# Ordering the attention output's small matrix products by tile size, and issuing two scalar loads from GpSimd

## The chip, the cores and the metric

The kernel runs on one core of one Trainium2 chip. The metric is the device time of one execution in microseconds. A core has the engines TensorE (PE in the profile, its weight loads PEld), VectorE (DVE), ScalarE (ACT), GpSimd (POOL) and SyncE (SP), which here issues nearly all DMA transfers.

## What is computed

A gated linear attention with a running 48 x 48 state per head is followed by a two-layer network with a squared ReLU. There are 4 batches of 8 heads, 768 steps, 48 channels a head; the network takes the 3072 x 384 result through a 2048-wide layer and back.

```python
for t in range(S):
    state = alpha[:, :, t, :, None] * state + einsum('bhd,bhe->bhde', k[:, :, t], v[:, :, t])
    y[:, :, t] = einsum('bhd,bhde->bhe', q[:, :, t], state)
x = y.transpose(0, 2, 1, 3).reshape(B * S, H * D)      # 3072 x 384
r = maximum(x @ w_in, 0)
out = (s * (r * r) + b) @ w_out                        # s and b are scalars
```

## The kernel before

**Blocks.** The 768 steps of a batch are cut into 6 chunks of 128, so there are 24 blocks of 128 steps (blocks 0, 6, 12 and 18 open a batch and have no state yet). For each block the attention runs through these steps:

- `load` (L175): four DMA transfers (alpha, q, k, v) into rings of 5 buffers, issued from SP.
- `st_ln` (L275, ACT): logarithm of alpha into one of two buffers `la`. `st_cum` (L281, L286, PE): running sums over the block into the PSUM tile `ct_ps`. `st_exp_b`, `st_exp_i` (L295 to L299, ACT): exponentials `b_s`, `binv`, `blast`.
- `st_qb`, `st_kb` (L308, L313, DVE): scaled q and k. `st_T` (L324, PE): eight transposes, `st_Tcopy` (L344, DVE) copies them out to `qkT`.
- `st_vcast` (L302, POOL): v in bf16 into one of three buffers `vp`. `st_KV` (L335, PE): eight products of k and v into the PSUM tile `py_ps`. `st_t1` (L354, L356, DVE) and `st_snew` (L364, POOL): the next state `s_st`.
- `st_A` (L370, PE): eight products of k and q into `a_ps`. `st_mask` (L379, DVE): the causal mask, into `am`.
- `st_y` (L409, L419, PE): the block's output, transposed, into `py_ps`. `st_yevac` (L433, ACT): copies it to `xd`.

**The y products.** The output of 4 pairs of 96 channels lies as 384 channels in 12 strips of 32 PSUM partitions (strip x is in column block x // 4, at partition 32 * (x % 4)). A pair of heads fills 3 strips, so its products are 64 and 32 columns wide. `S_PARTS` lists the 8 products of the state with q (L409, left out where the block opens a batch) and `V_PARTS` the 12 products of v with the masked scores (L419). In order, the widths are 64, 32, 32, 64, 64, 32, 32, 64 for the state, and 64, 32, 32, 64, 64, 32, 32, 64, 32, 32, 32, 32 for v. Each product has a weight load of its own (128 rows, 64 or 32 columns) and streams 128 columns.

**The network.** Blocks are gathered in groups (2, 2, 2, 2, 4, 4, 4, 4 blocks). `mm1` (L455, PE) writes into `h_ps`, `relu` (L464, ACT) and `square` (L472, DVE) follow, `mm2` (L479, PE) accumulates into `o_ps`, `oevac` (L490, DVE) applies s and the bias row, and `ostore` (L502, SP) writes out. The bias row is b times the column sums of w_out: `colsum_part` and `colsum_add` (L247, L252, DVE), `bias_mul` (L255, L256, POOL, which waits for `b_col`) and `bias_mm` (L262, PE).

**What sets the order.** Every step is entered in a planner (`Schedule`) with an engine, an estimated duration, a priority and the data it reads and writes. The planner runs the list with these estimates, and each engine's instructions are emitted in the order that comes out; on the chip each engine then keeps to that order. For loads, the planner knows that block 0's four inputs come at 3.5 to 6.5 us (`sched.done`, L527), and takes 0.98 us of SP time and 2 us of latency for each later load. The `st_y` of a block stands in it at 0.6 us (L582). The output stores stand on SP too, in the order in which the planner sees them become ready.

Of the kernel before, what the change touches and what calls it, by code (L numbers as in the profile page):

```python
# [114 lines left out]
def kernel(  # L115
# [12 lines left out]
    nc = tc.nc  # L128
# [23 lines left out]
    y_ps = py_ps[:, 0:384].rearrange("a (k t) -> a k t", k=3)  # L152
# [17 lines left out]
    s_col = sb.tile([128, 1], FP32, name="s_col")  # L170
# [219 lines left out]
    def quadrant(x):  # L390
        return x // 4, 32 * (x % 4)

    S_PARTS = [(0, 0, 2), (0, 2, 1), (1, 3, 1), (1, 4, 2), (2, 6, 2), (2, 8, 1), (3, 9, 1), (3, 10, 2)]
    V_PARTS = [
        (0, 0, 0, 2), (0, 1, 2, 1), (1, 0, 3, 1), (1, 1, 4, 2), (2, 0, 6, 2), (2, 1, 8, 1),
        (3, 0, 9, 1), (3, 1, 10, 2), (0, 1, 1, 1), (1, 0, 4, 1), (2, 1, 7, 1), (3, 0, 10, 1),
    ]

    def st_y(n):
        first = n % NCH == 0  # L400
        qT = qkT_sb[n % 2][:, 0]
        am = am_sb[n % 2]
        vp = vp_sb[n % 3]
        st = s_sb[(n - 1) % 2]
        if not first:
            for p, x, m in S_PARTS:
                kk, r0 = quadrant(x)
                c0 = 32 * x - 96 * p
                nc.tensor.matmul(  # L409
                    out=y_ps[r0 : r0 + 32 * m, kk, :],  # L410
                    lhsT=st[:, p, c0 : c0 + 32 * m],
                    rhs=qT[:, p, :],
                    start=(x < 4),
                    stop=False,
                )
        for i, (p, e, x, m) in enumerate(V_PARTS):
            kk, r0 = quadrant(x)
            c0 = 32 * x - 96 * p + 48 * e
            nc.tensor.matmul(  # L419
                out=y_ps[r0 : r0 + 32 * m, kk, :],  # L420
                lhsT=vp[:, p, c0 : c0 + 32 * m],
                rhs=am[:, e, p, :],
                start=(first and i < 3),
                stop=(i >= 8),
            )
# [80 lines left out]
    op = sched.op  # L506
# [15 lines left out]
    for rank, item in enumerate(loads):  # L522
        t, i = rank - 1000, int(item[1:])
        if item[0] == "b":
            if i == 0:
                for x, name in enumerate("aqkv"):
                    sched.done((name, 0), 3.5 + x)  # L527
                op("SP", 0.5, t + 0.5,
                   lambda: nc.sync.dma_start(out=b_col, in_=moe_b.to_broadcast((128, 1))),
                   w=["b"], lat=2.0)  # L530
                op("SP", 0.5, t + 0.6,
                   lambda: nc.sync.dma_start(out=s_col, in_=moe_s.to_broadcast((128, 1))),
# [3 lines left out]
        st = stage % NST  # L536
# [15 lines left out]
    for g in range(NG):  # L552
        m = GROUPS[g]
        ring = [(first_blk[g] + x) % RING for x in range(m)]
        for n in range(first_blk[g], first_blk[g] + m):
# [26 lines left out]
            op("PE", 0.6, t + 0.7, st_y, n, r=rr, w=["py"], lat=0.27)  # L582
# [57 lines left out]
```

## Time and profile before

| | us |
|---|---|
| median of 3 runs | 233.87 |
| lowest, highest | 233.66, 234.86 |
| the profiled execution's own time | 235.56 |
| its span in the profile | 233.8 |
| TensorE busy in the span | 211.7 |
| VectorE busy | 144.0 |
| ScalarE busy | 100.8 |
| GpSimd busy | 45.4 |

The profile is of one execution on the one core. Its page lists the busy time of each engine, the span in 40 slices, and the chain of work that ended last, followed back from the last instruction. Other views give instructions in order of time (start, duration, engine, line, what is written from what, count; several alike in a row are merged), the busy time of each engine in chosen stretches (with the number of its instructions that lie in the stretch in brackets), and who waited for whom. A duration of a matrix product is from its start to the modelled end of its drain, so products overlap in the rows, and the distance between starts is what a product costs TensorE.

### The profile page before, as it was taken

Reading aid. Unit: us, or ns where it says so; the run is one execution under the profiler, and the core shown is the slowest. Engines: PE = TensorE matmul, PEld = TensorE weight load, DVE = VectorE, ACT = ScalarE, POOL = GpSimd, SP = SyncE. Lnnn points to the kernel's source line nnn. Section 1 sums busy time; section 2 is a strip of 40 time slices with the busy share of each in tenths; the row PEclk is TensorE's granted clock in tenths of the full one; section 3 lists DMA queues with packets and bytes.
Section 4 is the critical chain, followed back from the end, with each engine's and each line's share of the span. In section 5 each row is a group of like instructions: output and inputs, shape, how many; then the busy total and the mean of one; then the engine's idle time right before and its main releaser. Section 6 shows DMA issues by size and latency. Waiting matters only on the chain.

```text
span 233.8 us, 4929 instructions
## 1 busy us (share of the span) xinstructions
PE 211.7 (91%) x1916; PEld 123.9 (53%) x1916; DVE 144.0 (62%) x283; ACT 100.8 (43%) x217; POOL 45.4 (19%) x63
## 2 busy tenths in 40 slices
PE   0268696799999999999999999999999999999993
PEld 0134473466676666655555555545555555555562
DVE  2266459998779666675767865597656754343321
ACT  3213351554565534523656545675354433444300
POOL 5234439333102220200202120001210100000000
PEclk9999999799999999999999999999999999999999
DMA  6999798995789989689895464300000100101111
GB/s 135 184 289 249 199 366 197 242 205 111 157 171 213 192 190 185 143 172 215 170 181 101 97 146 104 67 3 34 35 3 34 36 0 34 36 35 38 64 70 67
DMA packets 107320, 30.21 MB, mean 129 GB/s; under 512 B 100640, under 2 KB 105760, under 8 KB 107296
## 3 DMA queue, kind: packets, MB, share of 16 engines
q1 hardware_dynamic: 107296, 29.89, 55.2%
q8 instruction: 15, 0.25, 0.5%
q14 instruction: 9, 0.07, 0.1%
HBM read 25.17 MB, written 4.72 MB: 128 GB/s over the span
## 4 chain that ended last, share of the span: by engine, by line
PE 82%; SPq 7%; DVE 5%; DMA 3%; issue 1%; ACT 0%
PE h_ps_67 L455 14%; PE o_ps_69 L479 14%; PE h_ps_66 L455 14%; PE o_ps_68 L479 13%; PE py_ps L419 8%; PE py_ps L409 7%; SPq L175 5%; PE ct_ps L324 4%; PE a_ps L370 3%; PE py_ps L335 3%; DMA a_in_73<-in_alpha_dram 3%; PE ct_ps L281 2%; SPq L220 1%; DVE colpart L247 1%; DVE colsum L252 1%
## 5 line engine op out<-in xcount | busy, mean ns | idle before, releaser
L464 ACT ACTIVATE r_149<-h_ps_66 128x512 bf16<-128x512 f32 x48 | 28.7, 598 | 46.2 <-PE h_ps_66 L455 37.4
L455 PEld LDWEIGHTS <-w_in_bf 128*128 128x128 bf16 x384 | 34.9, 100 | 22.0 <-issue 2.1
L464 ACT ACTIVATE r_150<-h_ps_67 128x512 bf16<-128x512 f32 x48 | 28.7, 599 | 20.1 <-PE h_ps_67 L455 13.5
L455 PE MATMUL h_ps_66<-xd_147,w_in_bf 128*128 128x512 bf16 (+1 forms) x72 | 17.0, 357 | 0.0
L379 DVE TENSOR_TENSOR am_138<-a_ps,mask 128x1024 bf16<-128x1024 f32 x12 | 14.7, 1222 | 3.4 <-PE a_ps L370 3.2
L344 DVE COPY qkT_136<-ct_ps 128x1024 bf16<-128x1024 bf16 x12 | 8.3, 688 | 13.7 <-PE ct_ps L324 13.7
L455 PE MATMUL h_ps_67<-xd_147,w_in_bf 128*128 128x512 bf16 (+1 forms) x72 | 16.5, 348 | 0.0
L344 DVE COPY qkT_137<-ct_ps 128x1024 bf16<-128x1024 bf16 x12 | 8.3, 690 | 12.9 <-PE ct_ps L324 12.8
L379 DVE TENSOR_TENSOR am_139<-a_ps,mask 128x1024 bf16<-128x1024 f32 x12 | 14.7, 1221 | 2.3 <-PE a_ps L370 2.0
L455 PE MATMUL h_ps_67<-xd_146,w_in_bf 128*128 128x256 bf16 (+1 forms) x72 | 13.8, 321 | 1.5 <-ACT r_150 L464 1.5
L455 PE MATMUL h_ps_66<-xd_146,w_in_bf 128*128 128x256 bf16 (+1 forms) x72 | 13.9, 323 | 0.0
L364 POOL TENSOR_TENSOR s_st_144<-t_142,blast_140 128x384 bf16<-128x384 bf16 x8 | 7.7, 968 | 24.6 <-DVE t_142 L356 17.7
L433 ACT ACTIVATE xd_147<-py_ps 128x384 bf16<-128x384 f32 x10 | 4.9, 490 | 15.2 <-PE py_ps L419 15.2
L409 PE MATMUL py_ps<-qkT_137,s_st_144 128*64 128x128 bf16 (+1 forms) x96 | 11.4, 242 | 0.0
L324 PE MATMUL ct_ps<-ident_bf,qb_128 128*128 128x128 bf16 x48 | 5.1, 234 | 5.4 <-DVE qb_128 L308 5.4
L409 PEld LDWEIGHTS <-s_st_144 128*64 128x64 bf16 (+1 forms) x96 | 6.2, 101 | 6.9 <-issue 3.5
L455 PE MATMUL h_ps_66<-xd_148,w_in_bf 128*128 128x256 bf16 (+1 forms) x48 | 9.8, 327 | 0.0
L455 PE MATMUL h_ps_67<-xd_148,w_in_bf 128*128 128x256 bf16 (+1 forms) x48 | 9.8, 327 | 0.0
L364 POOL TENSOR_TENSOR s_st_145<-t_143,blast_141 128x384 bf16<-128x384 bf16 x8 | 7.0, 879 | 13.3 <-DVE t_143 L356 11.2
L419 PEld LDWEIGHTS <-vp_113 128*32 128x32 bf16 (+1 forms) x96 | 5.0, 99 | 6.3 <-issue 3.5
L281 PE MATMUL ct_ps<-la_97,U_bf 128*128 128x384 bf16 x12 | 4.5, 376 | 4.1 <-ACT la_97 L275 4.1
L295 ACT ACTIVATE b_s_125<-ct_ps 128x384 f32<-128x384 f32 x12 | 5.9, 489 | 5.4 <-PE ct_ps L286 5.1
(207 smaller groups left out, 480.8 us busy)
## 6 DMA issues: line engine op xcount, KB each, us to landing
out_dram<-o_sb_167 SPq DMA_DIRECT2D x8, 192.0 KB, 2.0
out_dram<-o_sb_168 SPq DMA_DIRECT2D x8, 192.0 KB, 2.0
out_dram<-o_sb_169 SPq DMA_DIRECT2D x8, 192.0 KB, 1.9
a_in_70<-in_alpha_dram SPq DMA_DIRECT2D x5, 192.0 KB, 4.2
q_in_75<-in_q_dram SPq DMA_DIRECT2D x5, 192.0 KB, 3.6
k_in_80<-in_k_dram SPq DMA_DIRECT2D x5, 192.0 KB, 3.9
v_in_85<-in_v_dram SPq DMA_DIRECT2D x5, 192.0 KB, 4.0
a_in_71<-in_alpha_dram SPq DMA_DIRECT2D x5, 192.0 KB, 3.6
```

What stands on the lines that cost most here:

```text
L175: nc.sync.dma_start(out=dst[n % NIN], in_=src[b, :, c * C : (c + 1) * C, :].rearrange("h s d -> s h d"),)
L281: nc.tensor.matmul(out=cum_ps, lhsT=U_bf, rhs=la[:, :, 0:D], start=True, stop=True)
L324: nc.tensor.transpose(out=t_ps[:, x, p, :], in_=f[:, 128 * p : 128 * p + 128], identity=ident_bf,)
L335: nc.tensor.matmul(out=p_ps[64 * e : 64 * e + 64, p, :], lhsT=kb[:, 128 * p + 64 * e : 128 * p + 64 * e + 64], rhs=vp[:, p, 48 * e : 48 * ...
L344: nc.vector.tensor_copy(out=qkT_sb[n % 2].rearrange("a x p t -> a (x p t)"), in_=t_ps.rearrange("a x p t -> a (x p t)"),)
L364: nc.gpsimd.tensor_tensor(out=s_sb[n % 2], in0=t1_sb[n % 2], in1=bl, op=ALU.mult)
L379: nc.vector.tensor_tensor(out=am_sb[n % 2].rearrange("a e p t -> a (e p) t"), in0=a_ps.rearrange("a e p t -> a (e p) t"), in1=mask.unsquee ...
L409: nc.tensor.matmul(out=y_ps[r0 : r0 + 32 * m, kk, :], lhsT=st[:, p, c0 : c0 + 32 * m], rhs=qT[:, p, :], start=(x < 4), stop=False,)
L419: nc.tensor.matmul(out=y_ps[r0 : r0 + 32 * m, kk, :], lhsT=vp[:, p, c0 : c0 + 32 * m], rhs=am[:, e, p, :], start=(first and i < 3), stop=( ...
L455: nc.tensor.matmul(out=hp[:, i * n : (i + 1) * n], lhsT=w_in_bf[:, kk, 128 * j : 128 * (j + 1)], rhs=xd_sb[g % 3][:, kk, 0:n], start=(kk = ...
L464: nc.scalar.activation(out=r_sb[w % 2], in_=h_ps[w % 2], func=AF.Relu)
L479: nc.tensor.matmul(out=op[:, 0:d_model], lhsT=gt_sb[j][:, c0 : c0 + C], rhs=w_out_bf[:, j, :], start=(j == 0), stop=(j == NJ - 1),)
```

## The change

The two lists become one, `Y_PARTS`, in which all products 64 columns wide come first (four of the state, four of v) and then all products 32 columns wide (four of the state, eight of v). Neighbours in the list go to different partitions: two products of 64 columns, or four of 32, fill the 128 output partitions. The products themselves, their number and their sizes stay. Which product starts the accumulation in a strip is now worked out from the order. The two loads of the scalars b and s are issued from GpSimd in place of SP, in the planner too, and the planner's estimate of `st_y` goes from 0.6 to 0.55 us.

```diff
-    S_PARTS = [(0, 0, 2), (0, 2, 1), (1, 3, 1), (1, 4, 2), (2, 6, 2), (2, 8, 1), (3, 9, 1), (3, 10, 2)]
-    V_PARTS = [
-        (0, 0, 0, 2), (0, 1, 2, 1), (1, 0, 3, 1), (1, 1, 4, 2), (2, 0, 6, 2), (2, 1, 8, 1),
-        (3, 0, 9, 1), (3, 1, 10, 2), (0, 1, 1, 1), (1, 0, 4, 1), (2, 1, 7, 1), (3, 0, 10, 1),
+    Y_PARTS = [
+        (0, None, 0, 2), (2, None, 6, 2), (1, None, 4, 2), (3, None, 10, 2),
+        (0, 0, 0, 2), (2, 0, 6, 2), (1, 1, 4, 2), (3, 1, 10, 2),
+        (2, None, 8, 1), (3, None, 9, 1), (0, None, 2, 1), (1, None, 3, 1),
+        (2, 1, 8, 1), (3, 0, 9, 1), (0, 1, 2, 1), (1, 0, 3, 1),
+        (1, 0, 4, 1), (0, 1, 1, 1), (3, 0, 10, 1), (2, 1, 7, 1),
     ]
...
+        parts = [x for x in Y_PARTS if not (first and x[1] is None)]
+        fresh = {0, 1, 2, 3}
+        for i, (p, e, x, m) in enumerate(parts):
+            c0 = 32 * x - 96 * p
+            mine = {(x + y) % 4 for y in range(m)}
+            start = mine <= fresh
+            fresh -= mine
...
-                op("SP", 0.5, t + 0.5,
-                   lambda: nc.sync.dma_start(out=b_col, in_=moe_b.to_broadcast((128, 1))),
+                op("POOL", 0.5, t + 0.5,
+                   lambda: nc.gpsimd.dma_start(out=b_col, in_=moe_b.to_broadcast((128, 1))),
                    w=["b"], lat=2.0)
-                op("SP", 0.5, t + 0.6,
-                   lambda: nc.sync.dma_start(out=s_col, in_=moe_s.to_broadcast((128, 1))),
+                op("POOL", 0.5, t + 0.6,
+                   lambda: nc.gpsimd.dma_start(out=s_col, in_=moe_s.to_broadcast((128, 1))),
                    w=["s"], lat=2.0)
...
-            op("PE", 0.6, t + 0.7, st_y, n, r=rr, w=["py"], lat=0.27)
+            op("PE", 0.55, t + 0.7, st_y, n, r=rr, w=["py"], lat=0.27)
```

Three places of the emitted order matter for the prediction. The first is TensorE at the y products of block 0, which opens a batch and has the 12 products of v alone; `vp_113` is its v, `am_138` its masked scores, and the last numbers are the output partitions by the streamed columns. Before, from its first product on:

```order
L419 LDWEIGHTS vp_113
L419 MATMUL py_ps<-am_138,vp_113 64x128
L419 LDWEIGHTS vp_113
L419 MATMUL py_ps<-am_138,vp_113 32x128
L419 LDWEIGHTS vp_113
L419 MATMUL py_ps<-am_138,vp_113 32x128
L419 LDWEIGHTS vp_113
L419 MATMUL py_ps<-am_138,vp_113 64x128
```

With the change, from the third product on (the two ahead of it are 64 wide as well):

```order
L414 LDWEIGHTS vp_113
L414 MATMUL py_ps<-am_138,vp_113 64x128
L414 LDWEIGHTS vp_113
L414 MATMUL py_ps<-am_138,vp_113 64x128
L414 LDWEIGHTS vp_113
L414 MATMUL py_ps<-am_138,vp_113 32x128
L414 LDWEIGHTS vp_113
L414 MATMUL py_ps<-am_138,vp_113 32x128
```

The width changed at every first, third and fifth product of a run of four; now it changes once in the block, after the last product that is 64 wide.

The second place is the start, on ACT, where `la_97` is the logarithm of block 0's alpha and `la_99` that of block 1's, and on POOL, where `vp_113` is block 0's v and `vp_115` block 1's. On ACT:

```order
-L635 UNCONDITIONAL_BRANCH
+L634 UNCONDITIONAL_BRANCH
 L184 ACT_TABLE_LOAD
+L275 ACTIVATE la_99<-a_in_71 128x8x48
 L275 ACTIVATE la_97<-a_in_70 128x8x48
```

On POOL:

```order
+L528 DMA b_col<-in_moe_b_dram 128x1
+L531 DMA s_col<-in_moe_s_dram 128x1
 L255 MEMSET bones 128x128
 L256 TENSOR_SCALAR bones<-bones,b_col 128x128
+L302 CAST vp_115<-v_in_86 128x4x2x48
 L302 CAST vp_113<-v_in_85 128x4x2x48
-L302 CAST vp_115<-v_in_86 128x4x2x48
```

The two loads stand ahead of the instruction that reads b, and on both engines block 1's step now stands ahead of block 0's, because the planner takes block 1's loads to land before block 0's.

The third place is SP's queue, around the store of block 1's output (`o_sb_168`) and the loads of block 9 (`a_in_74` to `v_in_89`) and block 10 (`a_in_70`). Before:

```order
L175 DMA v_in_88<-in_v_dram 128x8x48
L502 DMA out_dram<-o_sb_168 128x384
L175 DMA a_in_74<-in_alpha_dram 128x8x48
L175 DMA q_in_79<-in_q_dram 128x8x48
L175 DMA k_in_84<-in_k_dram 128x8x48
L175 DMA v_in_89<-in_v_dram 128x8x48
L175 DMA a_in_70<-in_alpha_dram 128x8x48
```

With the change:

```order
L175 DMA v_in_88<-in_v_dram 128x8x48
L175 DMA a_in_74<-in_alpha_dram 128x8x48
L175 DMA q_in_79<-in_q_dram 128x8x48
L175 DMA k_in_84<-in_k_dram 128x8x48
L175 DMA v_in_89<-in_v_dram 128x8x48
L175 DMA a_in_70<-in_alpha_dram 128x8x48
L501 DMA out_dram<-o_sb_168 128x384
```

The store moved behind five loads.

30 lines of the change are left out of this document (9 added, 21 removed).

## The prediction

> **What bounds the kernel now.** I read the page first (the span, the busy shares, the granted clock), then the chain of work that ended last, then the busy times of chosen stretches, then the instructions in order of time around one block's y products.
>
> ```profile
> span 233.8 us, 4929 instructions
> PE 211.7 (91%) x1916; PEld 123.9 (53%) x1916; DVE 144.0 (62%) x283; ACT 100.8 (43%) x217; POOL 45.4 (19%) x63
> PE h_ps_67 L455 14%; PE o_ps_69 L479 14%; PE h_ps_66 L455 14%; PE o_ps_68 L479 13%; PE py_ps L419 8%; PE py_ps L409 7%; SPq L175 5%; PE ct_ps L324 4%; PE a_ps L370 3%; PE py_ps L335 3%; DMA a_in_73<-in_alpha_dram 3%; PE ct_ps L281 2%; SPq L220 1%; DVE colpart L247 1%; DVE colsum L252 1%
> ```
>
> TensorE is busy for 91% of the span and makes up most of the chain. The y products (L409 and L419) are about 15% of it, some 35 us. The chain in order of time (start, duration, what) shows where TensorE starts to be the bound:
>
> ```profile
> 18.16 6.32 DMA a_in_73<-in_alpha_dram
> ...
> 30.46 0.85 PE py_ps L409 x8
> ...
> 41.29 1.13 DVE am_139 L379
> ...
> 49.49 0.76 PE h_ps_67 L455 x6
> ...
> 53.56 0.85 PE py_ps L409 x8
> ...
> 195.94 0.85 PE py_ps L409 x8
> ...
> 227.61 2.61 PE o_ps_69 L479 x16
> ```
>
> Up to 24.5 us the chain is SP and its transfers, then TensorE with block 2's y (30.46), then VectorE until some 49 us, and from 49.49 us on TensorE to the end. Blocks 4 (53.56) to 23 (195.94) have their y in that last stage: 20 blocks, of which 6, 12 and 18 open a batch, so 17 with 20 products and 3 with 12. What a y costs TensorE there is paid in full. Two stretches (columns: PE, PEld, DVE, ACT, POOL busy, granted clock, DMA share) show how much room the others have:
>
> ```profile
> 50.00:60.00 10.00, 10.00 (x105) 6.49 (x103) 9.17 (x23) 5.32 (x14) 3.75 (x4) 1.00 0.74 154
> ...
> 81.86:89.13 7.26, 7.26 (x80) 4.81 (x80) 5.06 (x13) 3.62 (x9) 1.33 (x2) 1.00 0.92 192
> ```
>
> The second is one block's period. VectorE works 5.06 of 7.26 us in it, ScalarE 3.62. In the first, just after the VectorE stage, VectorE has little room (9.17 of 10). The clock is granted in full.
>
> **What a y costs now.** In order of time, block 14's y (20 products) and what follows it, and block 6's y (12 products):
>
> ```profile
> 125.87 0.92 PE L409 MATMUL py_ps<-qkT_136,s_st_145 128*64 128x128 bf16 x8
> ...
> 127.57 0.82 PE L455 MATMUL h_ps_66<-xd_147,w_in_bf 128*128 128x512 bf16 x3
> ```
>
> ```profile
> 68.02 1.09 PE L419 MATMUL py_ps<-am_138,vp_113 128*64 128x128 bf16 x12
> 69.04 0.28 PE L455 MATMUL h_ps_67<-xd_148,w_in_bf 128*128 128x256 bf16 x1
> ```
>
> So a y costs 127.57 - 125.87 = 1.70 us, and 69.04 - 68.02 = 1.02 us in a block that opens a batch. Cutting block 14's y into stretches of 0.17 us shows how it comes about (the busy time and number of the weight loads, each of which goes with one product):
>
> ```profile
> 125.86:126.03 0.17, 0.11 (x1) 1.00 0.00 0
> 126.03:126.20 0.17, 0.10 (x2) 1.00 0.00 0
> 126.20:126.37 0.17, 0.11 (x2) 1.00 0.23 48
> ...
> 127.22:127.39 0.17, 0.11 (x1) 1.00 1.17 220
> 127.39:127.56 0.17, 0.10 (x4) 1.00 1.25 256
> ```
>
> The products go in 10 steps of 0.17 us: one 64 wide, two 32 wide, two 64 wide and so on to four 32 wide (the five stretches left out hold 2 each). Every step is a run of equal width, and the step costs 0.17 us whether it holds one product, two or four. Products of one width on different partitions run beside each other; where the width changes, TensorE stands. A block that opens a batch has 6 such steps, 6 x 0.17 = 1.02 us, as measured.
>
> What a step without a change of size costs is in the rows of the transposes and of the score products, all streaming 128 columns:
>
> ```profile
> 128.23 0.39 PE L324 MATMUL ct_ps<-ident_bf,qb_130 128*128 128x128 bf16 x4
> 128.45 0.39 PE L324 MATMUL ct_ps<-ident_bf,kb_134 128*128 128x128 bf16 x4
> ...
> 123.23 0.40 PE L370 MATMUL a_ps<-qkT_136 64*128 64x128 bf16 x8
> 123.56 0.34 PE L281 MATMUL ct_ps<-la_99,U_bf 128*128 128x384 bf16 x1
> ```
>
> Four transposes take 128.45 - 128.23 = 0.22 us, 0.055 us each. The eight score products take 0.33 us up to the next size: they go in four pairs, three steps of 0.055 and one of 0.165 us that holds the change. So 0.055 us is streaming and some 0.115 us the change of size.
>
> **The change part by part.**
>
> *The y order.* A full y becomes four pairs of 64 and then three rows of four 32: three steps of 0.055, one of 0.17 (64 to 32), two of 0.055, one of 0.17 (32 to the next size): 0.62 us. It saves 1.08 us. A y that opens a batch becomes two pairs and two rows of four: 0.055 + 0.17 + 0.055 + 0.17 = 0.45 us; it saves 0.57 us. In the last stage that is 17 x 1.08 + 3 x 0.57 = 20.1 us. The trace has a row of four 32-wide products only once in a block, with a change behind it; that three of them follow at 0.055 us each is taken over from the pairs. The bounds are 0.62 us and, if each of the seven steps cost 0.17 us, 7 x 0.17 = 1.19 us; I take 0.62, since the pairs are the nearest row. The Trainium skill speaks against it in one place: TensorE: Matmul & The Clock Gate, section "Wait — 56ns, not 53.3ns?", gives about 62 ns of sequencer time for each product with hardware decode off. By it 20 products take an estimated 1.24 us, and the sum would be 17 x 0.46 + 3 x 0.28 = 8.7 us. The score products above do not agree with it: 8 in 0.33 us, the change included, are 0.041 us each.
>
> *What comes next where TensorE is faster.* A block's period goes from 7.26 to about 6.2 us. VectorE's 5.06 us fit (82%). In the stretch from 50 to 60 us TensorE would need 10 - 1.08 = 8.9 us (block 4's y lies in it), while VectorE has 9.17 us to do: 0.3 us come back. For queueing behind VectorE elsewhere I add 0.9 us, a choice: 1.2 us, with bounds of 0 and 6 us (0.3 us for each of the 20 blocks).
>
> *The scalar loads and the start.* In order of time:
>
> ```profile
> 3.45 0.98 SPq L529 DMA_DIRECT2D b_col<-in_moe_b_dram  x1
> 3.49 0.52 ACT L275 ACTIVATE la_97<-a_in_70 128x384 bf16<-128x384 f32 x1 [1.50 <-DMA a_in_70<-in_alpha_dram]
> ...
> 4.34 0.29 PE L286 MATMUL ct_ps<-ones_col_bf,la_97 128*128 128x1 bf16 x4
> ...
> 5.11 0.60 SPq L175 DMA_DIRECT2D a_in_71<-in_alpha_dram  x1
> ...
> 7.48 0.50 POOL L302 CAST vp_113<-v_in_85 128x384 bf16<-128x384 f32 x1
> ...
> 8.46 0.52 ACT L275 ACTIVATE la_99<-a_in_71 128x384 bf16<-128x384 f32 x1 [4.45 <-DMA a_in_71<-in_alpha_dram]
> 8.89 0.47 ACT L295 ACTIVATE b_s_124<-ct_ps 128x384 f32<-128x384 f32 x1
> ...
> 11.02 0.53 PE L335 MATMUL py_ps<-vp_113,kb_132 128*64 128x96 bf16 x8
> 11.14 0.51 POOL L302 CAST vp_115<-v_in_86 128x384 bf16<-128x384 f32 x1 [3.16 <-DMA v_in_86<-in_v_dram]
> ```
>
> ```profile
> 5.00:6.00 1.00, 0.00 (x0) 0.00 (x0) 0.00 (x0) 0.00 (x0) 0.00 (x0) 1.00 0.58 107
> 6.00:7.00 1.00, 0.00 (x0) 0.00 (x0) 0.00 (x0) 0.00 (x0) 0.07 (x1) 1.00 0.36 52
> ```
>
> SP issues b and s from 3.45 us, and block 1's first load follows at 5.11: without them every later load moves up by up to 1.66 us. The transfers can use that only while they idle; from 5 to 7 us they are busy 0.58 and 0.36, so about 1.06 us of them is free. The early chain is SP and transfers, so I take 1.0 us. The bounds: 2.7 us gained (1.66 and block 2's 1.08, which stands on the chain at 30.46), and 1 us lost.
>
> Loss could come from the swapped steps. On ACT block 1's logarithm now stands ahead of block 0's. It waited for its load until 8.46; the exponential behind it came at 8.89, though block 0's sums were done by 4.63 (4.34 + 0.29). Now block 0's logarithm starts 0.43 us behind block 1's, and the exponential 1.1 us behind that (4.63 - 3.49): with the load 1.66 us earlier, 6.80 + 0.43 + 1.14 = 8.4 us, against 8.89. Nothing is lost while that load gains 1.1 us or more of its 1.66. On POOL, both casts of v now wait behind `bones`, which waits for b, and block 0's behind block 1's. Block 0's k-v products (11.02) need it. With v of block 1 some 1.5 us earlier, the casts end at about 10.6 us, so b has until some 9.5 us to land, 5.6 us after POOL reaches its issue at about 3.9. No row has a transfer issued from GpSimd; the nearest is SP's b, 0.98 us of issue. By DMA: Bandwidth & Descriptors, section "Anatomy of one DMA — SWDGE (gpsimd) path", of the Trainium skill a GpSimd transfer takes about 2.0 us fixed, an estimate of 6 us for the landing; no run here shows it yet. Either way it costs nothing.
>
> *The planner's order.* The loads of block 9 were the tightest in the last stage:
>
> ```profile
> 63.97 0.36 SPq L502 DMA_DIRECT2D out_dram<-o_sb_168  x1
> 64.42 0.38 SPq L175 DMA_DIRECT2D a_in_74<-in_alpha_dram  x1
> ...
> 68.67 0.51 ACT L275 ACTIVATE la_99<-a_in_74 128x384 bf16<-128x384 f32 x1
> ```
>
> The load went out behind the store at 64.42 and was used at 68.67. The new order puts five loads ahead of that store, so a shorter period does not run into it. I cost the reordering at nothing; where the tight loads came late after all, it is in the 6 us above.
>
> **The sum.** 20.1 + 1.0 - 1.2 = 19.9 us less. The profiled execution took 235.56 us, 1.8 more than its span, and would take 215.7. It lies 1.7 us above the median of the runs, 233.87; against that the forecast is 214.0 us. About 0.5%, 1.2 us, is what a measurement here can tell from no change.
>
> **The rivals.**
>
> *A. No row of products follows the next without a stall.* If the weights of a row of equal width are not loaded beside the row ahead, each of the seven steps costs 0.17 us: a y of 1.19 us saves 0.51, one that opens a batch (4 x 0.17 = 0.68) 0.34 us, 9.7 us in all, about 224. Against it stand the score products, whose pairs follow at 0.055 us; for it, that no three rows of four follow each other in the trace. A limit on how fast products are issued would show the same way, a y of over 1 us; its chance is in this one. Chance 0.10.
>
> *B. VectorE or the loads take over.* For it: 9.17 of 10 us at the start of the stage, and the load used 4.25 us after its issue. Against it: 5.06 of 7.26 us later, and the new SP order. At 0.2 to 0.35 us a block, 4 to 7 us come back: 218 to 221. Chance 0.14.
>
> *C. Slower: weight loads go one by one.* All y products use all 128 rows. The Trainium skill says (TensorE: Matmul & The Clock Gate, Part 3, "The mechanism") that a weight load overlaps running products only where the row group differs. Here it would work so: at about 0.10 us a load (the 0.10 and 0.11 of the stretches), 20 loads and two changes of 0.115 are 2.2 us a y, 0.5 us more than now, and 12 loads 1.4 us, 0.4 more: 17 x 0.5 + 3 x 0.4 = 10 us, about 243. It decides where a load costs over (1.70 - 0.23) / 20 = 0.073 us. Against it: four loads lie within 0.10 us in the last stretch, and the score products go at 0.041 us each. The trace thus does not agree with that rule for different columns. Chance 0.03.
>
> *D. Nothing to measure*, if VectorE bound the whole last stage at today's pace. Its 5.06 of 7.26 us speak against it. Chance 0.02, at 234.
>
> **How the numbers follow.** The forecast has 0.71: 214.0 us, with its own bounds about 210.5 (no time comes back, 2.7 us gained early: 233.87 - 20.1 - 2.7 = 211.1, and half a microsecond of spread) and 217. B reaches to 221. The range 210.5 to 221.5 holds the forecast and B, 0.85, less some at their edges; A, C and D lie outside. Faster: forecast, A and B, 0.95. Within 0.5%: 0.02. Slower: C, 0.03.
>
> **What would show it.** Right: after the change a y costs 0.6 to 0.65 us from its first product to the next line, with loads in one stretch of four pairs and one of twelve; PE's busy time falls by 20 us or more; TensorE still has no wait from some 50 us on; the first transfer of block 1 is issued at about 3.5 us. Wrong: a y over 0.8 us (A or C); waits of TensorE on `am`, `gt` or `a_in` between 50 and 190 us that add up to over 3 us (B); a first k-v product later than 11.5 us (the start lost, not gained).

## The result and the profile after

| | before | after |
|---|---|---|
| median, us | 234.06 (4 runs, 233.66 to 234.86) | 217.59 (4 runs, 215.89 to 220.06) |
| ratio, 95% interval | | 0.9268 [0.9207, 0.9329] |
| the profiled execution | 235.56, span 233.8 | 217.64, span 215.9 |

The changed kernel is 16.5 us faster by the medians; 19.9 us had been forecast, to 214.0. The run of 220.06 is left out of the ratio, and so is one of 983.64 us of after_again below, because each lies over 1.5% above the fastest run of its kernel.

From the page of the changed kernel, the span, the busy time of each engine and the granted clock in 40 slices:

```profile
span 215.9 us, 4933 instructions
PE 190.6 (88%) x1916; PEld 112.4 (52%) x1916; DVE 149.3 (69%) x283; ACT 100.8 (47%) x217; POOL 47.5 (22%) x65
PEclk9999998788999999999999999999999999999999
```

TensorE's busy time falls from 211.7 to 190.6 us, by 21.1. Its clock dips in slices 7 to 10, between 32 and 54 us.

In order of time, block 14's y (20 products) and what follows it:

```profile
118.92 0.30 PE L414 MATMUL py_ps<-qkT_136,s_st_145 128*64 128x128 bf16 x4
119.05 0.28 PE L414 MATMUL py_ps<-am_138,vp_117 128*64 128x128 bf16 x4
119.26 0.24 PE L414 MATMUL py_ps<-qkT_136,s_st_145 128*32 128x128 bf16 x4
119.33 0.28 PE L414 MATMUL py_ps<-am_138,vp_117 128*32 128x128 bf16 x8
119.55 0.61 PE L454 MATMUL h_ps_66<-xd_147,w_in_bf 128*128 128x512 bf16 x2
```

A full y takes 119.55 - 118.92 = 0.63 us, where it took 1.70. Its two halves are 0.34 (64 wide) and 0.29 us (32 wide).

The busy times in three stretches (columns as before: PE, PEld, DVE, ACT, POOL busy, granted clock, DMA share):

```profile
50.00:60.00 10.00, 10.00 (x113) 6.72 (x110) 9.30 (x23) 6.46 (x15) 3.02 (x4) 0.98 0.64 134
...
100.00:120.00 20.00, 19.78 (x225) 10.07 (x224) 17.66 (x33) 15.00 (x34) 4.14 (x6) 1.00 0.80 163
112.80:118.90 6.10, 6.10 (x69) 3.09 (x68) 5.09 (x11) 4.71 (x10) 1.61 (x2) 1.00 0.66 130
```

From 50 us on TensorE is the bound as before: in a block's period, now 6.10 us, it is busy all the time and VectorE 5.09 us. Of TensorE's waits only one lies behind 50 us, the 0.22 us that are missing between 100 and 120.

The start, in order of time:

```profile
3.75 0.86 SPq L175 DMA_DIRECT2D a_in_71<-in_alpha_dram  x1
3.83 0.74 POOL L528 DMA_DIRECT2D b_col<-in_moe_b_dram  x1
4.57 0.55 POOL L531 DMA_DIRECT2D s_col<-in_moe_s_dram  x1
...
7.21 0.61 POOL L256 TENSOR_SCALAR bones<-bones,b_col 128x128 f32<-128x128 f32 x1 [1.89 <-DMA b_col<-in_moe_b_dram]
...
8.13 0.52 ACT L275 ACTIVATE la_99<-a_in_71 128x384 bf16<-128x384 f32 x1 [6.13 <-DMA a_in_71<-in_alpha_dram]
...
9.72 0.49 ACT L295 ACTIVATE b_s_124<-ct_ps 128x384 f32<-128x384 f32 x1 [0.65 <-PE ct_ps L286]
...
11.58 0.50 POOL L302 CAST vp_113<-v_in_85 128x384 bf16<-128x384 f32 x1
...
12.13 0.53 PE L335 MATMUL py_ps<-vp_113,kb_132 128*64 128x96 bf16 x8 [0.20 <-POOL vp_113 L302]
```

```profile
5.00:6.00 1.00, 0.00 (x0) 0.00 (x0) 0.00 (x0) 0.00 (x0) 0.33 (x2) 1.00 0.93 181
6.00:7.00 1.00, 0.00 (x0) 0.00 (x0) 0.00 (x0) 0.00 (x0) 0.00 (x0) 1.00 0.90 172
```

Block 1's alpha load went out 1.36 us earlier (3.75 against 5.11), yet was used only 0.33 us earlier (8.13 against 8.46): the transfers, 0.58 and 0.36 busy between 5 and 7 us before, were now 0.93 and 0.90 busy. These are single executions, and y_issue below shows the same load gain more. Block 0's exponential, now behind block 1's logarithm, came 0.83 us later (9.72 against 8.89), and its first k-v products 1.1 us later (12.13 against 11.02).

So the y products are as forecast, and 3.4 us of the sum (19.9 - 16.5) are missing elsewhere. The theory at this point: the y order is worth what was forecast, and the move of the scalar loads, with the new order that the planner makes of it, costs time. The rivals: the y order gives less than its shorter products say, or the swapped steps at the start cost it.

### The profile page after: what moved, and what is told of

The parts are those of the page before. It is cut to its first block, busy times and chain, and to the rows that moved or that the text cites. A ratio compares the mean times of both kernels' runs of the same rounds, so it can differ in the third digit from the quotient of the medians.

```text
span 215.9 us, 4933 instructions
## 1 busy us (share of the span) xinstructions
PE 190.6 (88%) x1916; PEld 112.4 (52%) x1916; DVE 149.3 (69%) x283; ACT 100.8 (47%) x217; POOL 47.5 (22%) x65
## 4 chain that ended last, share of the span: by engine, by line
PE 51%; DVE 0%; issue 0%
PE o_ps_69 L478 10%; PE h_ps_66 L454 10%; PE o_ps_68 L478 10%; PE h_ps_67 L454 10%; PE py_ps L414 3%; PE ct_ps L324 2%; PE a_ps L370 2%; PE py_ps L335 2%; PE ct_ps L281 1%; PE ct_ps L286 0%; DVE o_sb_169 L489 0%
## 5 line engine op out<-in xcount | busy, mean ns | idle before, releaser
L454 PEld LDWEIGHTS <-w_in_bf 128*128 128x128 bf16 x384 | 36.0, 102 | 23.9 <-issue 3.1
L454 PE MATMUL h_ps_66<-xd_147,w_in_bf 128*128 128x512 bf16 (+1 forms) x72 | 16.3, 344 | 1.4 <-ACT r_149 L463 1.4
L454 PE MATMUL h_ps_67<-xd_147,w_in_bf 128*128 128x512 bf16 (+1 forms) x72 | 16.7, 352 | 0.0
L454 PE MATMUL h_ps_67<-xd_146,w_in_bf 128*128 128x256 bf16 (+1 forms) x72 | 14.4, 333 | 0.7 <-ACT r_150 L463 0.7
L454 PE MATMUL h_ps_66<-xd_146,w_in_bf 128*128 128x256 bf16 (+1 forms) x72 | 15.0, 344 | 0.0
L364 POOL TENSOR_TENSOR s_st_144<-t_142,blast_140 128x384 bf16<-128x384 bf16 x8 | 7.7, 960 | 23.5 <-DVE t_142 L356 16.3
L364 POOL TENSOR_TENSOR s_st_145<-t_143,blast_141 128x384 bf16<-128x384 bf16 x8 | 7.8, 974 | 15.4 <-DVE t_143 L356 13.3
L454 PE MATMUL h_ps_66<-xd_148,w_in_bf 128*128 128x256 bf16 (+1 forms) x48 | 9.8, 327 | 0.0
L454 PE MATMUL h_ps_67<-xd_148,w_in_bf 128*128 128x256 bf16 (+1 forms) x48 | 9.8, 326 | 0.0
L295 ACT ACTIVATE b_s_124<-ct_ps 128x384 f32<-128x384 f32 x12 | 5.9, 491 | 7.9 <-PE ct_ps L286 7.6
L295 ACT ACTIVATE b_s_125<-ct_ps 128x384 f32<-128x384 f32 x12 | 5.9, 490 | 6.1 <-PE ct_ps L286 5.8
L286 PEld LDWEIGHTS <-la_97 128*128 128x128 bf16 x48 | 3.1, 100 | 8.8 <-issue 8.0
L308 DVE TENSOR_TENSOR qb_128<-q_in_75,b_s_124 128x384 bf16<-128x384 f32 x3 | 1.7, 552 | 7.7 <-ACT b_s_124 L295 7.7
```

Source lines behind the costliest of these rows:

```text
L295: nc.scalar.activation(out=b_sb[n % 2], in_=cum_ps, func=AF.Exp)
L364: nc.gpsimd.tensor_tensor(out=s_sb[n % 2], in0=t1_sb[n % 2], in1=bl, op=ALU.mult)
L454: nc.tensor.matmul(out=hp[:, i * n : (i + 1) * n], lhsT=w_in_bf[:, kk, 128 * j : 128 * (j + 1)], rhs=xd_sb[g % 3][:, kk, 0:n], start=(kk = ...
```

## The experiments

Every ratio is to the kernel before, run on the same chip.

| kernel | median, us (runs) | ratio, 95% interval |
|---|---|---|
| y_only | 215.34 (6) | 0.9182 [0.9150, 0.9213] |
| scalars_only | 236.79 (6) | 1.0102 [1.0066, 1.0137] |
| start_pinned | 218.86 (4) | 0.9342 [0.9314, 0.9370] |
| y_sp055 | 215.34 (6) | 0.9191 [0.9153, 0.9228] |
| y_issue | 214.99 (6) | 0.9171 [0.9139, 0.9203] |
| no_colsum | 210.78 (6) | 0.9001 [0.8967, 0.9035] |
| three_changes_y | 218.73 (4) | 0.9335 [0.9299, 0.9372] |
| same_columns_y | 215.32 (4) | 0.9189 [0.9141, 0.9238] |
| after_again | 219.18 (6) | 0.9312 [0.9269, 0.9355] |
| after_no_colsum | 212.59 (6) | 0.9036 [0.8996, 0.9076] |
| bias_pe | 213.46 (6) | 0.9080 [0.9035, 0.9125] |
| clock_fill | 217.18 (6) | 0.9268 [0.9237, 0.9299] |

### The two halves of the change apart

**y_only** has the new `Y_PARTS` and `st_y`, with b and s on SP and the planner's 0.6 us for a y, so that every step stands where it stood before.

> The new y order alone: scalar loads on SP and the planner's 0.6 us as before, so every engine's order is that of the kernel before, but for the order inside a y. Theory 1 (the early loss of the changed kernel comes from what the planner reordered): no start is lost, a y costs 0.63 and 0.46 us, and the 17 x 1.07 + 3 x 0.56 = 19.9 us of the last stage are saved: 214 us. Rival 2 (a shorter y by itself leaves TensorE idle longer before 50 us, its clock is halved once more, and VectorE's stage stays as long): some 2 to 3 us of it are lost again, 216 to 217.5 us, with two stretches of granted clock 0.5 between 30 and 51 us as in the changed kernel, in place of one.

**scalars_only** is the other half, on the old y order (the edit for s is the same).

```diff
-                op("SP", 0.5, t + 0.5,
-                   lambda: nc.sync.dma_start(out=b_col, in_=moe_b.to_broadcast((128, 1))),
+                op("POOL", 0.5, t + 0.5,
+                   lambda: nc.gpsimd.dma_start(out=b_col, in_=moe_b.to_broadcast((128, 1))),
```

> The old y order, b and s issued from GpSimd, 0.6 us in the planner. Theory 1: the start (block 1's logarithm ahead of block 0's) and the reordering cost what the changed kernel lost early, 1 to 3 us: 235 to 237 us, with block 0's first exponential at 9.7 us in place of 8.9. Rival 2: the loss needs the short y, so within 1 us of before, 233 to 235 us. The prediction's own step (1 us gained by issuing block 1's loads earlier): 233 us.

**y_sp055** is the changed kernel with b and s back on SP; the planner's 0.55 us for a y stays.

> The changed kernel with b and s issued from SP again (planner's 0.55 us kept): the start is that of before, the later order is a third one. Theory 1: between 214 and 217 us, by what this order does to VectorE between 30 and 50 us. Rival 2: 216 to 217.5 us, like every kernel with the short y. If the GpSimd issue itself gained the predicted 1 us: 1 us slower than the pinned start.

**start_pinned** is the changed kernel with block 0's logarithm kept ahead of block 1's (and in the same way its cast of v).

```diff
-            op("ACT", 0.45, t - 1.0, st_ln, n, r=[("a", ii)], w=[("la", i2)])
+            op("ACT", 0.45, t - 1.0, st_ln, n, r=[("a", ii)] + ([("la", 0)] if n == 1 else []), w=[("la", i2)])
```

> The changed kernel, with block 0's logarithm and its cast of v kept ahead of block 1's; all later orders nearly as in the changed kernel. If the swapped start is the early loss: 1 to 2 us faster than the changed kernel, 215.5 to 216.5 us. If it is not (block 1's y already began 0.5 us earlier than before in the changed kernel's profile, so the start had caught up by 20 us): 217 to 218 us, the first exponential at about 5 us notwithstanding.

Measured: the y order alone takes 19.1 us off (234.46 to 215.34), more than the whole change. The scalar move adds 2.3 us to the old y order (1.0% [0.7%, 1.4%]) and about 2 us to the new one (0.9268 against 0.9182 and 0.9191). The planner's 0.55 us for a y changes nothing that can be measured (215.34 us with both). The swap at the start isn't what costs: pinned, the first k-v products start at 10.18 us instead of 12.13, and the kernel is no faster than the changed one. Its row:

```profile
10.18 0.53 PE L335 MATMUL py_ps<-vp,kb 128*64 128x96 bf16 x8
```

### The issue, or the order?

Moving the loads to GpSimd does two things: GpSimd issues them, and the planner, which books them there, gives nearly all engines another order. **y_issue** does the first alone. It is y_only with this edit (and the same for s), the planner still booking both on SP:

```diff
-                   lambda: nc.sync.dma_start(out=b_col, in_=moe_b.to_broadcast((128, 1))),
+                   lambda: nc.gpsimd.dma_start(out=b_col, in_=moe_b.to_broadcast((128, 1))),
```

> The kernel with the new y order alone, but the two scalar loads are issued from GpSimd, while the planner still books them on SP: every other step of every engine stays in its place. If the 2.3 us that the move of the scalar loads cost in scalars_only came from the planner's reordering, this kernel is as fast as y_only, 215.3 us, or up to 1 us faster, 214.3 (the prediction's term for the start: block 1's first load issued about 1.7 us earlier). If the GpSimd issue itself costs (the casts of v that stand behind it on GpSimd's queue, the first k-v products after them), it is 217 to 218 us, and the first k-v product comes 1 us later than in y_only. In both cases a y costs 0.62 us.

Measured: 214.99 us, 2.3 us below the changed kernel by the ratios (0.9268 - 0.9171, times 234; by the intervals 0.7 to 3.9), and not to be told from y_only. Against after_again, the changed kernel once more, it is 3.3 us (2.0 to 4.6). The issue from GpSimd costs nothing; the order costs. Nor does the start bring the forecast microsecond. Block 1's first load is issued at 3.59 us instead of y_only's 5.12 and used at 7.68 instead of 9.18, and the first k-v products come at 10.24 us instead of 11.74; yet block 1's y starts at 20.53 instead of 20.71, and the time moves by 0.3 us, less than the intervals tell. Block 1's k-v products wait until ScalarE has copied out block 0's y, and on ScalarE that copy stands behind block 2's logarithm, whose load comes only 0.19 us earlier. That logarithm in y_only and in y_issue:

```profile
18.24 0.52 ACT L275 ACTIVATE la<-a_in 128x384 bf16<-128x384 f32 x1 [3.47 <-DMA a_in<-in_alpha_dram]
```

```profile
18.05 0.52 ACT L275 ACTIVATE la<-a_in 128x384 bf16<-128x384 f32 x1 [4.79 <-DMA a_in<-in_alpha_dram]
```

What the order costs is seen from block 5's y, the first y well inside the stage that TensorE bounds. Its rows in before, the changed kernel, y_only and y_issue:

```profile
60.76 0.92 PE L409 MATMUL py_ps<-qkT_137,s_st_144 128*64 128x128 bf16 x8
```

```profile
60.10 0.30 PE L414 MATMUL py_ps<-qkT_137,s_st_144 128*64 128x128 bf16 x4
```

```profile
59.57 0.30 PE L414 MATMUL py_ps<-qkT,s_st 128*64 128x128 bf16 x4
```

```profile
59.30 0.30 PE L414 MATMUL py_ps<-qkT,s_st 128*64 128x128 bf16 x4
```

It starts at 59 to 61 us in all of them, although the five y's ahead of it are 4.8 us shorter together in the last three (4 x 1.07 + 0.56), and y_issue's k-v products start 1.5 us earlier. Each row is of one execution: before's took 1.7 us more than its median, and same_columns_y, a kernel in y_only's order that follows below, has this y at 57.56 us. From there to the end of the span (233.8, 215.9, 213.7 and 213.4 us) it is 173.0 us before, 155.8 in the changed kernel and 154.1 in y_only and y_issue. Counted in the traces, 389 TensorE products start ahead of it in the changed kernel and 399 in before, y_only and y_issue: six of `mm1` (0.66 us) and four of `mm2` (0.65 us) are done behind it instead. So the order leaves 1.3 us of TensorE work for the stage that TensorE bounds, and that stage starts 0.8 us later: 2.1 us of the 2.5 by which its span differs from y_issue's. The first of the two is the firmer: start_pinned and clock_fill (below), in the changed kernel's order, also take 155.8 us from there to the end, and y_sp055, with 399 products ahead, 154.6, while the start of the stage differs by more than 0.8 us between executions of one order. One sign of why it may start later: with the same 283 instructions VectorE is busy for 149.3, 150.3 and 149.8 us in the changed kernel, start_pinned and clock_fill, and for 146.0 and 146.4 in y_only and y_issue. That this is the reason is not shown.

### What holds block 5 at 60 us

**no_colsum** is y_only without the seven additions of the column sums of w_out on VectorE; a memset to zero stands for them, and the bias row is zero.

```diff
-        dst = colpart if i else colsum
-        nc.vector.tensor_tensor(
-            out=dst, in0=wst[st][:, 0 : QW // 2], in1=wst[st][:, QW // 2 : QW], op=ALU.add
-        )
+        if i == 0:
+            nc.vector.memset(colsum, 0.0)
...
-        nc.vector.tensor_tensor(out=colsum, in0=colsum, in1=colpart, op=ALU.add)
+        pass
```

> The kernel with the new y order alone; the seven VectorE additions that form the column sums of w_out are left out and one memset to zero stands for them, so that the bias row is zero in this kernel. It asks why block 5's y starts at about 60 us in every kernel, however long the y products ahead of it take. If VectorE's work from 32 to 50 us sets it, the seven additions of 1.5 to 2.2 us each are off that path: block 5's y at 55 to 57 us and 210 to 212 us in all. If the transfers set it, block 5's y stays at 59.6 us and the time at 215.3 us, to within 0.6.

Measured: 210.78 us, and block 5's y at 53.25. (In y_only the seven additions take 0.94 to 1.58 us each, less than the expectation has.) The stretch from 32 to 50 us of the changed kernel, then of y_issue, and of no_colsum, whose y of block 5 follows:

```profile
32.00:50.00 18.00, 11.87 (x104) 7.02 (x102) 17.77 (x27) 5.51 (x12) 8.84 (x6) 0.82 0.98 236
```

```profile
32.00:50.00 18.00, 12.24 (x140) 8.47 (x138) 17.61 (x28) 6.82 (x14) 9.24 (x8) 1.00 1.00 250
```

```profile
32.00:50.00 18.00, 16.01 (x190) 11.22 (x188) 14.81 (x34) 9.60 (x21) 8.42 (x8) 1.00 1.06 245
```

```profile
53.25 0.30 PE L412 MATMUL py_ps<-qkT,s_st 128*64 128x128 bf16 x4
```

VectorE is busy for 17.6 to 17.8 of these 18 us; with the additions gone 14.81, and TensorE gets 190 products done instead of 140. The transfers are as busy in all of them (their share about 1). The chain of work that ended last, here that of y_issue, goes through VectorE alone from 33.82 us up to block 4's y:

```profile
33.82 0.68 DVE qkT L344
...
52.04 1.15 DVE am L379
53.23 0.58 PE py_ps L414 x16
```

So it is VectorE that sets when TensorE becomes the bound.

**after_no_colsum** leaves out the same additions in the changed kernel's order, and **after_again** is the changed kernel itself beside it.

> The changed kernel without the seven VectorE additions of the column sums of w_out (a memset to zero stands for them, so the bias row is zero). If the 2.3 us that the planner's reordering costs all arise in VectorE's crowded stretch of 32 to 58 us, they vanish with the crowd: 210.8 us, like no_colsum. If the reordering leaves more TensorE work behind block 5's y whatever VectorE does, about 1.6 us of them stay: 212.4; if all stay, 213.1.

> The changed kernel once more, on the chip of the next two runs, so that they can be set against it directly. By the earlier runs it takes 217.6 us, 2 to 3 us more than the kernel with the new y order alone (215.3), of which some 1.6 us is TensorE work that the planner leaves for later than block 5's y and the rest VectorE's crowded stretch before it.

Measured: 0.9036 and 0.9312. Without the crowd on VectorE the order costs 0.0035 [-0.0017, 0.0087], 0.8 us (-0.4 to 2.0) against no_colsum, where with it it costs 2.3 to 3.3. The cost seems to shrink, which speaks for the crowd, but the intervals overlap; whether all of it goes, or the 1.3 us of deferred work stay, is not told apart.

**bias_pe** computes everything: it is y_issue with the column sums made by TensorE. `bones` holds ones, b is multiplied in where the bias row is copied, and VectorE's seven additions are gone.

```diff
-        for e in range(2):
+        for j in range(16):
             nc.tensor.matmul(
                 out=o_ps[1][:, 0:d_model],
                 lhsT=bones,
-                rhs=colsum[:, d_model * e : d_model * (e + 1)],
-                start=(e == 0),
-                stop=(e == 1),
+                rhs=w_out_bf[:, j],
+                start=(j == 0),
+                stop=(j == 15),
             )
```

> A version that computes everything: the kernel with the new y order and the scalar loads on GpSimd in the old order, with the column sums moved from VectorE to TensorE (16 products of a tile of ones with the bf16 tiles of w_out, 16 x 0.16 = 2.6 us, for the two f32 products that take some 2 us now; b is multiplied in where the bias row is copied). If VectorE's stretch from 32 to 58 us sets when TensorE becomes the bound, block 5's y moves from 59.3 to about 53.5 us and the time is 211 to 212 us. If something else takes over at once (the transfers, GpSimd's casts), it stays at 213.5 us or above.

Its stretch from 32 to 50 us, and its y of block 5:

```profile
32.00:50.00 18.00, 16.11 (x176) 11.61 (x174) 15.66 (x34) 9.91 (x21) 9.01 (x9) 1.00 1.08 251
```

```profile
57.43 0.30 PE L413 MATMUL py_ps<-qkT,s_st 128*64 128x128 bf16 x4
```

Measured: 213.46 us, a ratio of 0.9080, the fastest of the kernels that compute everything: 1.0% below y_issue and 2.0% below the changed kernel. The direction is as expected, the size is not: the median lies where the expectation put the rival (213.5), and block 5's y comes at 57.43 us, not 53.5, with VectorE at 15.66 of 18 us. The planner ordered this kernel anew, so its order is a second difference: 12 products of `mm2` more (2.0 us) stand ahead of block 5's y than in y_issue, and from there to the end it is 152.2 us instead of 154.1. In its trace the chain that ended last is TensorE alone as far back as it goes, to 40.2 us, so VectorE no longer sets the start of that stage.

### Not the clock

In all four runs of the changed kernel the mean granted clock was 0.965 to 0.984, in the other runs of after_again 0.973 to 0.984, in start_pinned's 0.958 to 0.984; in the kernels of the old order mostly 0.99 to 1. So a second theory: the new order lets TensorE idle, its clock is halved for it, and that is the loss. The changed kernel has two stretches of 3.4 us at half rate (second and fourth row, the clock in the third column from the end), each behind one in which TensorE was busy for only 0.98 or 1.02 of 3.40 us:

```profile
33.20:36.60 3.40, 0.98 (x4) 0.30 (x4) 3.40 (x5) 0.38 (x1) 2.79 (x2) 1.00 1.11 306
36.70:40.10 3.40, 3.23 (x21) 2.00 (x21) 3.40 (x5) 0.61 (x2) 2.42 (x2) 0.50 0.82 145
43.50:46.90 3.40, 1.02 (x10) 0.69 (x9) 3.40 (x6) 1.04 (x3) 1.62 (x1) 1.00 0.95 185
46.90:50.30 3.40, 3.39 (x25) 1.92 (x23) 3.40 (x11) 1.50 (x3) 0.00 (x0) 0.50 0.91 178
```

VectorE is busy for all of the 3.40 us in each of the four. **clock_fill** puts 63 idle products into those waits.

```diff
+    def fill(count):
+        for _ in range(count):
+            nc.tensor.matmul(
+                out=o_ps[1][:, 384:512], lhsT=ident_bf, rhs=U_bf, start=True, stop=True
+            )
+    FILL = {("st_T", 4): 12, ("mm2", 0): 20, ("mm1", 5): 3, ("mm1", 7): 4, ("mm1", 8): 16}
...
+            fill(8 if x == 0 and j == 3 else 0)
```

> The changed kernel with 63 more TensorE products of 128 x 128 (the identity by a triangle of ones, into unused columns of an output bank; nobody reads them) ahead of five of the places where TensorE waits between 32 and 47 us: 3.5 us of work in waits of 0.35 to 2.2 us each, every other step in its place. In all runs of the changed kernel the mean granted clock is 0.965 to 0.984, which is 2 to 4 stretches of 3.4 us at half rate; in those of the kernel with the new y order in the old order of steps it is mostly 0.992 to 1. If these stretches are where the 2 to 3 us are lost, and they come from TensorE idling ahead of them, the mean clock is 0.99 or more here and the time 215 to 216 us, a ratio of about 0.92. If the planner's order itself loses them (steps of TensorE left for later), the clock rises and the time stays at 217.6 to 219, a ratio of 0.927 to 0.931. If the clock doesn't rise, the idling is not what lowers it.

The same four stretches in clock_fill:

```profile
33.20:36.60 3.40, 2.66 (x40) 2.10 (x39) 3.40 (x3) 0.00 (x0) 3.40 (x2) 1.00 1.13 335
36.70:40.10 3.40, 2.73 (x26) 1.73 (x26) 3.40 (x8) 1.08 (x2) 1.71 (x3) 1.00 0.92 158
43.50:46.90 3.40, 1.71 (x36) 1.28 (x33) 3.40 (x5) 1.75 (x5) 1.62 (x1) 1.00 0.85 173
46.90:50.30 3.40, 3.14 (x41) 2.61 (x41) 3.40 (x11) 1.71 (x4) 0.00 (x0) 1.00 0.98 187
```

Measured: the half-rate stretches are gone, the mean clock is 0.997 to 1 in all six runs, and the ratio is 0.9268 [0.9237, 0.9299], that of the changed kernel to the fourth digit, and 1.0 us (-0.2 to 2.3) below that of after_again. With the clock full the kernel still stands 2.3 us (1.2 to 3.3) above y_issue, so the theory of the clock falls as the main cause; a smaller share of the loss is not excluded. y_only says so from the other side: in its profiled execution the granted clock from 32 to 50 us is 0.81, as low as the changed kernel's 0.82, and it took 215.51 us. TensorE runs slowly there while VectorE is busy all the time, and it is VectorE's work that the chain of y_issue goes through. How much the filled products cost by themselves was not measured.

### What a y product costs

**three_changes_y** is y_only with the four 64 wide v products behind the four 32 wide state products, so that the size changes two times more.

> The kernel with the new y order alone, but with each full y in four groups: state products 64 wide, state products 32 wide, v products 64 wide, v products 32 wide; a y that opens a batch is as before. Two more changes of size. By the prediction's sum a y is 3 x 0.055 + 4 x 0.17 = 0.85 us, 0.22 us more, in 17 blocks 3.8 us: 219.1 us. If what the old order paid was not the number of changes but its leftover single steps, it stays near 0.62 us and 215.3. If each of the seven rows costs 0.17 us as soon as rows are short, 1.2 us and 225.

Block 14's y in order of time (the first row holds all eight state products, the second all twelve of v):

```profile
117.71 0.47 PE L414 MATMUL py_ps<-qkT,s_st 128*64 128x128 bf16 x8
118.12 0.53 PE L414 MATMUL py_ps<-am,vp 128*64 128x128 bf16 x12
118.58 0.39 PE L454 MATMUL h_ps<-xd,w_in_bf 128*128 128x512 bf16 x1
```

Measured: a y of 118.58 - 117.71 = 0.87 us and 218.73 us in all; 0.85 and 219.1 were expected. Two more changes cost 0.24 us, 0.12 us each. From block 5's y on they are paid 16 times, 3.8 us by the rows; the medians differ by 3.4.

**same_columns_y** keeps one change of size, but lists the products so that those on the same columns follow each other (which product ends an accumulation follows from that order).

```diff
-        (0, None, 0, 2), (2, None, 6, 2), (1, None, 4, 2), (3, None, 10, 2),
-        (0, 0, 0, 2), (2, 0, 6, 2), (1, 1, 4, 2), (3, 1, 10, 2),
+        (0, None, 0, 2), (1, None, 4, 2), (0, 0, 0, 2), (1, 1, 4, 2),
+        (2, None, 6, 2), (3, None, 10, 2), (2, 0, 6, 2), (3, 1, 10, 2),
...
+        (2, None, 8, 1), (2, 1, 8, 1), (1, 0, 4, 1),
+        (3, None, 9, 1), (3, 0, 9, 1), (0, 1, 1, 1),
```

> The kernel with the new y order alone, with the same single change of size inside a y, but products that use the same columns of the array follow each other, two by two in the 64 wide part and three or two in the 32 wide part, so that fewer neighbours can run beside each other. If each product that follows another on its columns is a step of 0.055 us and only the change of size costs 0.17, a full y is about 1.1 us (14 steps and two changes) and a batch opener 0.67: 17 x 0.49 + 3 x 0.22 = 9 us more, 224.3. If a change of columns costs like a change of size, 1.6 us and 231. If only the number of size changes matters, 0.62 us and 215.3.

Block 15's y in order of time:

```profile
120.47 0.31 PE L415 MATMUL py_ps<-qkT,s_st 128*64 128x128 bf16 x4
120.60 0.29 PE L415 MATMUL py_ps<-am,vp 128*64 128x128 bf16 x4
120.82 0.26 PE L415 MATMUL py_ps<-qkT,s_st 128*32 128x128 bf16 x4
120.89 0.31 PE L415 MATMUL py_ps<-am,vp 128*32 128x128 bf16 x8
121.12 0.34 PE L479 MATMUL o_ps<-w_out_bf,gt 128*128 128x384 bf16 x1
```

Measured: 0.65 us a y, and 215.32 us, as y_only. The forecast of 224.3 by steps of neighbours was wrong; of the two orders' differences only the number of size changes counts. The rows show how. In the program the order is two state products, two v products (all on columns 0 to 63), then two state and two v products on columns 64 to 127. On the chip all four state products start first: the second columns' products don't wait for their neighbours ahead of them.

## Why the prediction was right, and where it was not

- **What bounds the kernel.** Right. TensorE bounds it from some 50 us on, before and after, and its busy time fell by 21.1 us (20 or more was named).
- **The y products.** Right to 0.01 us: 0.63 us measured for a full y, 0.62 forecast, and 0.46 for one that opens a batch, 0.45 forecast. That a change of size costs some 0.115 us and a row of equal width 0.055 was tested by three_changes_y (0.87 for 0.85). From block 5's y to the end the old order takes 173.0 us and y_only 154.1: 18.9 us, and 16 full y's at 1.07 and 3 at 0.56 are 18.8. The TensorEngine Tiling (Array Packing) page of the Trainium skill says, under "Key Properties", that a change of tiling mode drains TensorE while different tiles work in parallel; the trace agrees, at 0.12 us a change.
- **The reading of it.** In part wrong: "Products of one width on different partitions run beside each other" is true, but they needn't be neighbours, as same_columns_y shows. The part of the change that pairs neighbours on different columns earned nothing; the grouping by size did.
- **What is given back.** The size was right, the place in part by luck. The y order alone was to save 20.1 - 1.2 = 18.9 us and saved 19.1. The prediction took block 4's y as paid in full, less 0.3 us, and added 0.9 us for "queueing behind VectorE elsewhere", a choice. In the runs the last stage has no such queueing; what is lost is lost ahead of it. The y's of blocks 0 to 4 lie in or ahead of VectorE's crowded stretch, and of their 4.8 us only 1.2 show at block 5's y in y_only (59.57 against 60.76), where single executions differ by as much.
- **The start: a gain that does not reach the end.** "The early chain is SP and transfers, so I take 1.0 us." The first load of block 1 was issued at 3.75 us (3.5 named). In y_issue the load and the first k-v products did gain 1.5 us against y_only; by block 1's y 0.18 us of it was left, since block 2's load came hardly earlier. In the changed kernel the gain went in the swapped steps and in a load that landed 0.45 us later than y_issue's: the condition written there, nothing lost while the load gains 1.1 us or more, was not met in its trace (0.33 us), and its first exponential came at 9.72 us, where y_issue's came at 8.11. The mark set for a lost start (a first k-v product later than 11.5 us) came true at 12.13, but y_only, which starts like before, passes it too (11.74). Neither gain nor loss shows in the time: start_pinned, with its k-v products at 10.18, is no faster.
- **The planner's order: the step that failed.** "I cost the reordering at nothing." It costs the 2.0 to 2.3 us by which the changed kernel stands above y_only and y_issue. The prediction looked at the order of the loads in the last stage, and did not count what the new order leaves for that stage: ten products, 1.3 us. In scalars_only the same cause is not shown: there 8 products more stand ahead of block 5's y, which comes later (62.1 us), and its profiled execution, the fastest of its six, has the span of before's, which took 1.7 us more than its median.
- **The rivals.** A: no, y costs 0.63, not 1.19 us. At 0.031 us a product the trace lies below the 62 ns that TensorE: Matmul & The Clock Gate of the Trainium skill gives with hardware decode off ("Wait — 56ns, not 53.3ns?"); no run here shows which setting was in force. B: not in the last stage (VectorE 5.09 of 6.10 us in a period, no wait to add up); it holds ahead of 50 us. C: no. The section of the Trainium skill that speaks for it (TensorE: Matmul & The Clock Gate, "The mechanism") also says that products start strictly in the order of the program; same_columns_y doesn't agree with that for different columns. D: no.
- **The sum.** 20.1 - 1.2 stands as 19.1 measured; +1.0 at the start became 0.3 in y_issue, which can't be told from nothing, and the order took 2.3 back. That makes 17.1; the medians give 16.5 and the ratio 17.1 (0.0732 times 234). The time of 217.59 us lies 3.6 above the forecast and above its own bound of 217. It is inside the range only through the room made for rival B, whose cause (0.2 to 0.35 us lost in every block) is not the one that the runs show, and that much is luck.

## What to carry to other kernels

Where products of several tile sizes follow each other on TensorE, count the changes of size, not the products: group by size, and leave the order inside a group free. A change of queue that a planner books is two changes, the move and the new order; compare the program's orders by counting what each leaves for the stage that the bound engine fills, and test the move alone. A gain at the start is worth nothing while a later load, or a stage that another engine fills, sets when the bound engine's stage begins.

## What the runs showed of the hardware

**VectorE waits for GpSimd's casts.** In order of time, GpSimd's casts of w_out and VectorE's squares in the changed kernel:

```profile
32.26 2.26 POOL L240 CAST w_out_bf<-wst_172 128x1536 bf16<-128x1536 f32 x1 [0.60 <-DMA wst_172<-in_moe_w_out_dram]
...
33.11 1.55 DVE L471 TENSOR_TENSOR gt_153<-r_150 128x256 bf16<-128x256 bf16 x1
34.47 1.52 POOL L240 CAST w_out_bf<-wst_173 128x1536 bf16<-128x1536 f32 x1
...
34.58 1.54 DVE L471 TENSOR_TENSOR gt_154<-r_150 128x256 bf16<-128x256 bf16 x1
...
36.05 0.28 DVE L471 TENSOR_TENSOR gt_155<-r_149 128x256 bf16<-128x256 bf16 x1
```

The same square takes 0.28 us alone and 1.55 beside a cast, ending 0.1 us behind the cast's end (34.66 and 34.52; 36.12 and 35.99). The SBUF — State Buffer page of the Trainium skill, "SBUF: two separate sides", says that VectorE operations with two SBUF inputs and GpSimd lock one pair of ports for a whole instruction; the trace agrees. So part of VectorE's crowd is waiting that its busy time hides. No run here removed the casts.

**A load issued from GpSimd.** Its two issues took 0.74 and 0.55 us, and b was used 3.4 us after its issue started (7.21 and 3.83). That is later than the landing at 6 us that the prediction estimated, and well ahead of the 9.5 us by which it was needed there.

**An execution of 984 us.** The profiled execution of after_again took 983.64 us. In it TensorE's `mm2` products took 1354 ns in the mean instead of 327, at a granted clock shown as 1.0. It happened once, and nothing here explains it.
